# Another order of work around the first expert group of a gated recurrence with four experts

## The chip, the core and the metric

The kernel runs on one core of a Trainium2 chip. The metric is the device time of one launch in microseconds (us): the median over several runs. The engines are TensorE (PE in the profile; PEld is its loading of weights), VectorE (DVE), ScalarE (ACT), GpSimd (POOL) and SyncE (SP), which here only issues DMAs. Each works through its own instructions in order and waits for others by semaphores.

## The reference

Two parts follow each other. The first is a recurrence over time with a matrix as its state (2 batches, 8 heads, 768 steps, 40 features a head); the second feeds its output to four experts, and every expert sees every token.

```python
# recurrence, one step t for every batch and head
m_new  = maximum(f_gate + m, i_gate)
f_stab = exp(f_gate + m - m_new);  i_stab = exp(i_gate - m_new)
C = f_stab * C + i_stab * outer(vt, kt)
n = f_stab * n + i_stab * kt
y[t] = sigmoid(o_gate) * (C @ qt) / maximum(abs(n @ qt), 1.0)
# experts, x is y as 1536 tokens x 320 features
p = domain_probs / (domain_probs.sum(-1) + 1e-9)
out = sum over 4 experts e of  p[:, e] * (relu(x @ w1[e]) @ w2[e])    # hidden width 1024
```

## The kernel before

**Tiling.** The recurrence is computed in 12 chunks of 128 steps (6 a batch; chunk `n` belongs to batch `n % 2`). Within a chunk it is like attention: `scores(n)` (line 435) makes k times q for all heads on TensorE, `weigh(n)` (443) multiplies them on VectorE with decays, `intra(n)` (499) multiplies the weights with the values. What earlier chunks carry comes in by the state: `inter(n)` (480) multiplies q with it, eight ScalarE copies scale the result into `yb` (495), `norm(n)` (508) adds the two on VectorE, applies the output gate and divides. `state(n)` (449) makes the chunk's own part of the state; `carry(n)` (471) scales the old state on GpSimd. `turn(n)` (525) transposes the output on TensorE and ScalarE copies its rounded high part into `xst`; `turn_lo(n)` (535) writes the remainder with VectorE.

**Decays.** `decay(n)` (411) is a VectorE scan over `fb`, the forget factors spread over all partitions. For the first four chunks TensorE spreads them (`spread`, 392); from chunk 4 on a DMA does (`load_f`, 403). The gates themselves are a small chain: `gate_max`, `gate_f`, `gate_i`, `gate_b` (303, a VectorE scan and a ScalarE copy), `gate_t` (320, TensorE transposes of it, copied by ScalarE into `ibT`), `gate_last` (335, GpSimd), `gate_l` (344, TensorE spreads the last values, copied into `bl`). `values(n)` (421) scales the values on GpSimd with `ibT`, and ScalarE writes one more column; `keys(n)` (428) scales the keys on GpSimd. `gate_o(j)` (385) is the sigmoid on ScalarE of two chunks' output gates; it needs another activation table than the exponentials.

**Experts.** For accuracy each of x, w1, w2 is split into a rounded high part and a remainder (`quarter_hi`, `quarter_lo`, `split_w2_hi`, `split_w2_lo`: high on ScalarE, low on GpSimd). `hidden` (152) multiplies 256 tokens with two blocks of w1 in 16 products, then ScalarE writes the relu's high part and VectorE its low part. `output` (191) multiplies with w2. The first expert's work on the first 1024 tokens is cut into four groups of 256 tokens, each a list of steps: four hidden steps and then output steps. The first group has four output steps (high parts of w2 for two tiles of 128 tokens, then low parts), the others two. `steps(n)` (542) emits the next n steps. So expert steps are put by hand between the pieces of the recurrence, where TensorE would otherwise wait.

**Order.** There is no scheduler: the order in which the Python lines run is the order on every engine, and SyncE issues the DMAs in that order too. Lines 548 to 665 are a prologue written out by hand for chunks 0 to 3 and the first four hidden steps; the loop from 667 on does chunks 2 to 11 and takes its number of expert steps at three places of an iteration from `SLOTS` (38): before `inter`, after `weigh(n+1)` and `carry(n+1)`, and a third beside the transposes. Behind the loop come the other tokens and experts, nothing but dense products on TensorE. PSUM buffers come from pools of two: `ps_h` (hidden), `ps_o` (output and spreading), `ps_w` (scores), `ps_y` (chunk outputs, state products, transposes); the next use of a buffer waits for its last reader.

**Zero products.** `keep_warm(n)` (72) multiplies zeros, 128x128 with 128xn, into a buffer nobody reads.

Of the kernel before, what the change touches and what calls it, by code (L numbers as in the profile page):

```python
# [35 lines left out]
NPE = 4  # L36

SLOTS = (
    (0, 2, 0), (1, 1, 0), (1, 1, 0), (1, 1, 0), (1, 1, 0),
    (1, 1, 0), (1, 1, 0), (1, 1, 0), (1, 1, 1), (1, 1, 1),  # L40
)
PAD = 56
# [6 lines left out]
def tile_mlstm_moe(ctx, tc, gt, qk, vk, ot, dp, w1, w2, out):  # L49
# [22 lines left out]
    def keep_warm(n, pool=ps_h, tag="ph"):  # L72

        pwm = pool.tile([L, n], F32, tag=tag, name="pwm")
        nc.tensor.matmul(pwm, zero[:, 0:L], zero[:, 0:n], start=True, stop=True)  # L75
# [32 lines left out]
    def split_w2_hi(ws, f0, n, raw):  # L108
        f = slice(f0, f0 + n)
        split_hi(ws[:, HI, f], raw[:, f])  # L110

    def split_w2_lo(ws, f0, n, raw, eng):
        f = slice(f0, f0 + n)
        split_lo(ws[:, LO, f], ws[:, HI, f], raw[:, f], eng)
# [107 lines left out]
    with ExitStack() as actx:  # L222
# [7 lines left out]
        def quarter_hi(i):  # L230
            f, (ab, c) = slice(i * G, (i + 1) * G), w1r[i]
            split_hi(w1s[:, 0:2, f], ab)
            split_hi(w1s[:, 2, f], c)
# [151 lines left out]
        def gate_o(j):  # L385
            og = acc[:, 2 * j:2 * j + 2]
            nc.scalar.activation(og, og, AF.Sigmoid)
# [4 lines left out]
        def spread(n, pool, tag):  # L392

            b, c, k = n % B, n // B, 48 if n < B else L
            fbs[n] = [pool.tile([L, 4, L], F32, tag=tag, name="fb") for _ in range(2)]
            for h in range(H):
                nc.tensor.matmul(  # L397
                    fbs[n][h // 4][:, h % 4, :],
                    sel[0:k, b * H + h:b * H + h + 1].to_broadcast([k, L]),
                    fr[0:k, c * L:(c + 1) * L], start=True, stop=True,  # L400
                )
# [9 lines left out]
        def decay(n):  # L411
            dds[n] = a1.tile([L, H, L], F32, tag=f"dd{n % 2}", name="dd")
            for i in range(2):
                nc.vector.tensor_tensor_scan(  # L414
                    out=dds[n][:, 4 * i:4 * i + 4].rearrange("p h t -> p (h t)"),
                    data0=fbs[n][i].rearrange("p h t -> p (h t)"),
                    data1=id4.rearrange("p h t -> p (h t)"),
                    initial=0.0, op0=ALU.mult, op1=ALU.add,
                )

        def values(n):
            b, c = n % B, n // B
            vv = vvs[n] = vp[n % 2]
            iec = ibT[:, c, b * H:(b + 1) * H].unsqueeze(2)
            nc.gpsimd.tensor_mul(vv[:, :, 0:D], vks[n // 2][:, n % 2, 0], iec.to_broadcast([L, H, D]))
            nc.scalar.activation(vv[:, :, D:D + 1], iec, AF.Copy)

        def keys(n):
            if n // B < NC - 1:
                nc.gpsimd.tensor_mul(  # L430
                    kp[n % 2][:, :, 0:D], vks[n // 2][:, n % 2, 1],
                    dds[n][:, :, L - 1:L].to_broadcast([L, H, D]),
                )

        def scores(n, pool=ps_w, tag="w"):
            ss[n] = [pool.tile([L, NP, L], F32, tag=tag, name="s") for _ in range(2)]
            qg, kg = qT(n), kT(n)
            for p in range(NP):
                for r in range(2):
                    q = slice(64 * r, 64 + D * r)  # L440
                    nc.tensor.matmul(ss[n][r][:, p, :], kg[q, p], qg[q, p], start=True, stop=True)  # L441
# [100 lines left out]
        def steps(n):  # L542
            for _ in range(n):
                if not work[0].step():
                    work.pop(0)
# [36 lines left out]
        nc.scalar.activation(even, par.unsqueeze(2).to_broadcast([L, 2, 64]), AF.Copy)  # L582
        gate_max(1, NC)
        spread(0, ps_h, "ph")
        scores(0)
        gate_t(0, 1)
        pits.pop(0)
        gate_o(0)
        spread(1, ps_o, "po")
        g1, m1, mp1 = slice(L, S), mb[:, L + 1:S + 1], mb[:, L:S]  # L590
        nc.gpsimd.tensor_add(fs[:, g1], gat[:, 0, g1], mp1)
        decay(0)
        values(0)
        nc.gpsimd.tensor_sub(fs[:, g1], fs[:, g1], m1)
        nc.scalar.activation(fs[:, g1], fs[:, g1], AF.Exp)
        scores(1, ps_h, "ph")
# [9 lines left out]
        nc.sync.dma_start(w2r, w2[0])  # L606
        load_vk(1)
        load_o(1)
        keep_warm(512, ps_w, "w")
        keep_warm(512, ps_w, "w")  # L610
        weigh(1)
        quarter_hi(0)
        quarter_lo(0)
# [8 lines left out]
        turn_lo(1)  # L622
        quarter_lo(1)
        quarter_hi(2)
        keys(0)
        keys(1)
        quarter_lo(2)
        quarter_hi(3)
        quarter_lo(3)
        decay(2)  # L630
        steps(1)
        scores(2)
        weigh(2)
        state(0)
        state(1)
        gate_b(1, NC)
        gate_last(1, NC)
        steps(1)
        spread(3, ps_o, "po")
        decay(3)  # L640
        gate_t(1, NC)
        gate_l(1, NC)
        psum_e = const.tile([L, NCH, 1], F32, name="psum_e")
        nc.gpsimd.tensor_add(psum_e, pw[:, :, 0:1], pw[:, :, 1:2])
        for e in range(2, NE):
            nc.gpsimd.tensor_add(psum_e, psum_e, pw[:, :, e:e + 1])
        nc.gpsimd.tensor_scalar_add(psum_e, psum_e, 1e-9)
        for f in (0, 2):
            split_w2_hi(w2s, f, 2, w2r)
        values(2)  # L650
        carry(2)
        split_w2_lo(w2s, 0, 2, w2r, nc.gpsimd)
        keys(2)
        steps(1)
        for f in (4, 6):
            split_w2_hi(w2s, f, 2, w2r)
        split_w2_lo(w2s, 2, 2, w2r, nc.gpsimd)
        nc.vector.reciprocal(psum_e, psum_e)
        gctx.close()
        a0 = actx.enter_context(  # L660
            tc.tile_pool(name="a0", bufs=1, side="right", reuse_waits="tile")
        )
        load_f(NPE)
        steps(1)
        gate_o(1)

        for n in range(2, NCH):
            j, cc = n // 2, n % 2
            k = SLOTS[n - 2]
            nxt = n + 1 < NCH  # L670
            if cc == 0 and j + 1 < NG:
                load_qk(j + 1)
                load_vk(j + 1)
            if NPE < n + 2 < NCH:
                load_f(n + 2)
            if cc == 0:
                if j > 1:
                    gate_o(j)
                if j + 1 < NG:
                    load_o(j + 1)  # L680
            if n == NCH - 2:
                raw1 = load_w1e(1)
            if n > 2 and nxt:
                decay(n + 1)
            steps(k[0])
            inter(n)
            intra(n)
            norm(n)
            if nxt:
                scores(n + 1)  # L690
            state(n)
            if nxt:
                values(n + 1)
                keys(n + 1)
                weigh(n + 1)
                carry(n + 1)
            if n == 2:
                nc.gpsimd.tensor_mul(pw, pw, psum_e.to_broadcast([L, NCH, NE]))
                for f in (4, 6):
                    split_w2_lo(w2s, f, 2, w2r, nc.gpsimd)  # L700
            steps(k[1])
            if cc == 0:
                steps(k[2])
            turn(n)
            turn_lo(n)
            if cc == 1:
                steps(k[2])
# [109 lines left out]
```

## Time and profile before

| what | value |
|---|---|
| median of 3 runs | 412.97 us (411.39 to 413.19) |
| profiled execution | 414.57 us, its span 412.8 us |
| mean granted TensorE clock | 0.982 |
| PE busy | 403.8 us, 98% of the span |
| DVE busy | 173.6 us, 42% |
| ACT busy | 125.6 us, 30% |
| POOL busy | 82.0 us, 20% |
| DMA | 29.34 MB |

The span runs from the first to the last instruction; the execution's time is a little longer. Busy shares are means over the whole span: the first 60 us, which the change touches, look different from the rest. The profile gives a granted clock for TensorE as a share of 2.4 GHz; at 0.50 the engine runs at 1.2 GHz.

### The profile page before, as it was taken

How to read it: one execution, taken by the hardware profiler on the slowest of the kernel's cores; microseconds unless marked ns; L12 is line 12 of the kernel's file. 1: busy time of each engine (PE TensorE's matmuls, PEld its weight loads, DVE VectorE, ACT ScalarE, POOL GpSimd, SP SyncE). 2: the span in 40 equal slices, each digit the busy share in tenths (PEclk: the TensorE clock that was granted, in tenths of full speed). 3: DMA queues.
4: the chain of work that ended last, by engine and by line, in shares of the span. 5: the costliest groups of instructions: out<-in, count | busy, mean ns of one | idle time of the engine just before them, and what ended most of it. 6: DMA issues, size and time to landing. Idle time of an engine off the chain costs nothing.

```text
span 412.8 us, 7149 instructions
## 1 busy us (share of the span) xinstructions
PE 403.8 (98%) x3036; PEld 364.8 (88%) x3036; DVE 173.6 (42%) x312; ACT 125.6 (30%) x298; POOL 82.0 (20%) x97
## 2 busy tenths in 40 slices
PE   8998999999999999999999999999999999999996
PEld 5788979999998898998988988989989889889896
DVE  8573789798862403313214134133142251231321
ACT  4557334353333533205213033034031140120210
POOL 4849242222011720002510010006100010000000
PEclk9598999999999999999999999999999999999999
DMA  6949095577000112100300004002100000001001
GB/s 175 320 187 253 22 261 117 169 183 253 2 2 2 45 82 91 63 2 0 129 0 2 0 2 152 2 0 74 56 0 2 0 2 32 33 0 49 17 17 48
DMA packets 14884, 29.34 MB, mean 71 GB/s; under 512 B 988, under 2 KB 10748, under 8 KB 13436
## 3 DMA queue, kind: packets, MB, share of 16 engines
q1 hardware_dynamic: 14851, 28.88, 22.5%
q8 instruction: 24, 0.39, 0.4%
q14 instruction: 9, 0.07, 0.1%
HBM read 26.86 MB, written 2.02 MB: 70 GB/s over the span
## 4 chain that ended last, share of the span: by engine, by line
PE 91%; DVE 3%; POOL 2%; DMA 1%; issue 1%; ACT 0%; SPq 0%; DVEq 0%; POOLq 0%
PE po L203 41%; PE ph L164 37%; PE y L503 3%; PE ph L186 3%; PE s L441 3%; PE y L488 2%; DMA qk<-in_qk 1%; POOL w2s L99 1%; PE pwm L75 1%; PE px L530 1%; PE st L459 1%; DVE dd L414 1%; POOL cd L475 0%; DVE pm L447 0%; PE fb L397 0%
## 5 line engine op out<-in xcount | busy, mean ns | idle before, releaser
L203 PE MATMUL po<-w2s,h 128*128 128x320 f32 x1152 | 172.8, 310 | 0.0
L203 PEld LDWEIGHTS po<-w2s,h 128*128 128x128 f32 x1152 | 169.7, 188 | 1.0
L164 PE MATMUL ph<-xst,w1s 128*128 128x512 f32 (+1 forms) x816 | 166.3, 362 | 1.3 <-ACT xst L532 0.9
L164 PEld LDWEIGHTS ph<-xst,w1s 128*128 128x128 f32 x816 | 137.5, 191 | 26.5 <-issue 2.4
L173 ACT ACTIVATE h<-ph 128x512 fp32r<-128x512 f32 x96 | 57.4, 598 | 199.5 <-PE ph L164 199.5
L174 DVE SCALAR_TENSOR_TENSOR h<-ph,h 128x512 fp32r<-128x512 f32 x96 | 66.2, 690 | 104.9 <-ACT h L173 104.4
L213 DVE SCALAR_TENSOR_TENSOR acc<-po,pw,acc 128x320 f32<-128x320 f32 x36 | 19.8, 550 | 99.9 <-PE po L203 99.9
L99 POOL TENSOR_TENSOR w1s<-raw,w1s 128x512 fp32r<-128x512 f32 (+1 forms) x24 | 23.6, 1035 | 74.4 <-ACT w1s L96 67.4
L99 POOL TENSOR_TENSOR w2s<-raw,w2s 128x640 fp32r<-128x640 f32 x6 | 9.5, 1578 | 98.1 <-ACT w2s L96 98.1
L414 DVE TENSOR_TENSOR_SCAN dd<-fb,id 128x512 f32<-128x512 f32 x24 | 28.0, 1209 | 0.3
L495 ACT ACTIVATE yb<-y,ibT 128x41 f32<-128x41 f32 x80 | 16.0, 312 | 2.4 <-PE y L488 2.4
L211 ACT ACTIVATE acc<-po,pw 128x320 f32<-128x320 f32 x12 | 6.3, 528 | 31.7 <-PE po L203 31.7
L441 PE MATMUL s<-qk 64*128 64x128 f32 (+1 forms) x192 | 15.0, 297 | 1.0 <-DMA qk<-in_qk 1.0
L447 DVE TENSOR_TENSOR pm<-s,dd 128x512 f32<-128x512 f32 x24 | 15.4, 686 | 0.6 <-PE s L441 0.3
L503 PEld LDWEIGHTS y<-vp,pm 128*64 128x64 f32 x384 | 13.6, 148 | 1.7 <-issue 1.5
L430 POOL TENSOR_TENSOR kp<-vk,dd 128x320 f32<-128x320 f32 x10 | 7.3, 736 | 37.1 <-DVE dd L414 37.1
L503 PE MATMUL y<-vp,pm 128*64 128x41 f32 x384 | 14.2, 237 | 0.0
L441 PEld LDWEIGHTS s<-qk 64*128 64x128 f32 (+1 forms) x192 | 12.6, 199 | 1.7 <-DMA qk<-in_qk 1.1
L96 ACT ACTIVATE w2s<-raw 128x640 fp32r<-128x640 f32 x12 | 8.8, 733 | 16.4 <-DMA raw<-in_w 16.4
L186 PE MATMUL ph<-xd,w1s 64*128 64x512 f32 x40 | 12.0, 419 | 0.0
L186 PE MATMUL ph<-xst,w1s 64*128 64x512 f32 x40 | 11.9, 417 | 0.0
L96 ACT ACTIVATE w1s<-raw 128x512 fp32r<-128x512 f32 (+1 forms) x24 | 11.2, 516 | 0.0
(90 smaller groups left out, 199.4 us busy)
## 6 DMA issues: line engine op xcount, KB each, us to landing
raw<-in_w SPq DMA_DIRECT2D x3, 1536.0 KB, 6.5
qk<-in_qk SPq DMA_DIRECT2D x5, 832.0 KB
fb<-f_d SPq DMA_DIRECT2D x8, 512.0 KB, 7.1
raw<-in_w SPq DMA_DIRECT2D x3, 1280.0 KB
vk<-in_vk SPq DMA_DIRECT2D x5, 640.0 KB, 9.3
acc<-in_ot SPq DMA_DIRECT2D x6, 320.0 KB, 8.8
out<-acc SPq DMA_DIRECT2D x12, 160.0 KB, 1.8
w2r<-in_w SPq DMA_DIRECT2D x1, 1280.0 KB
```

The costliest lines, as they stand in the source:

```text
L96: nc.scalar.activation(hi, raw, AF.Copy)
L99: eng.tensor_sub(lo, raw, hi.bitcast(F32))
L164: nc.tensor.matmul(ph[:, i, :], self.w1s[:, wi, f * L:(f + 1) * L], xst[:, xi, self.t0:self.t0 + n], start=(k == 0 and not self.wide), sto ...
L173: nc.scalar.activation(hh, ph, AF.Relu)
L174: nc.vector.scalar_tensor_tensor(out=hl, in0=ph, scalar=0.0, in1=hh.bitcast(F32), op0=ALU.max, op1=ALU.subtract)
L186: nc.tensor.matmul(self.banks[f][:, 0, :], self.w1s[r, 5, f * L:(f + 1) * L], x, start=True, stop=False,)
L203: nc.tensor.matmul(po, self.hs[f][a][:, sl], ws[:, b, f, :], start=(first and i == 0), stop=(last and i == len(ks) - 1),)
L213: nc.vector.scalar_tensor_tensor(out=acc[:, i, :], in0=po, scalar=pw[:, i, e:e + 1], in1=acc[:, i, :], op0=ALU.mult, op1=ALU.add,)
L414: nc.vector.tensor_tensor_scan(out=dds[n][:, 4 * i:4 * i + 4].rearrange("p h t -> p (h t)"), data0=fbs[n][i].rearrange("p h t -> p (h t)") ...
L441: nc.tensor.matmul(ss[n][r][:, p, :], kg[q, p], qg[q, p], start=True, stop=True)
L495: nc.scalar.activation(yb[:, h], y1[:, h, 0:D + 1], AF.Copy, scale=ibT[:, c, i:i + 1])
L503: nc.tensor.matmul(y[t, h, 0:D + 1], pms[n][:, h, t], vvs[n][:, h, 0:D + 1], start=True, stop=True,)
```

## The change

Nothing that is computed changes, apart from zero products; instructions are emitted in another order. Two zero products of 256 columns are added between `spread(0)` and `scores(0)`. The two of 512 columns ahead of `intra(1)` become three of 256. `values(0)` stands ahead of `gate_o(0)` (and so its ScalarE column ahead of the sigmoid). `quarter_hi(3)` is called ahead of `keys(0)` and `keys(1)`. `gate_b` and `gate_last` come ahead of the first hidden step, `decay(2)` behind it; `weigh(2)` behind the two states. `gate_t` comes ahead of `spread(3)`, and `gate_l` behind the third hidden step. `gate_o(1)`, `values(2)` and `keys(2)` come ahead of that step. `psum_e`, the sum of the probabilities on GpSimd, comes behind the first low parts of w2 and `carry(2)`, and its reciprocal on VectorE behind the fourth hidden step. The second pair of w2 high parts moves into the loop, behind `norm(2)`. In `SLOTS` chunk 4 takes both its expert steps after its attention.

```diff
--- before.py
+++ after.py
@@ -36,7 +36,7 @@
 NPE = 4
 
 SLOTS = (
-    (0, 2, 0), (1, 1, 0), (1, 1, 0), (1, 1, 0), (1, 1, 0),
+    (0, 2, 0), (1, 1, 0), (0, 2, 0), (1, 1, 0), (1, 1, 0),
     (1, 1, 0), (1, 1, 0), (1, 1, 0), (1, 1, 1), (1, 1, 1),
 )
 PAD = 56
@@ -582,15 +582,17 @@
         nc.scalar.activation(even, par.unsqueeze(2).to_broadcast([L, 2, 64]), AF.Copy)
         gate_max(1, NC)
         spread(0, ps_h, "ph")
+        for _ in range(2):
+            keep_warm(256, ps_w, "w")
         scores(0)
         gate_t(0, 1)
         pits.pop(0)
+        g1, m1, mp1 = slice(L, S), mb[:, L + 1:S + 1], mb[:, L:S]
+        nc.gpsimd.tensor_add(fs[:, g1], gat[:, 0, g1], mp1)
+        values(0)
         gate_o(0)
         spread(1, ps_o, "po")
-        g1, m1, mp1 = slice(L, S), mb[:, L + 1:S + 1], mb[:, L:S]
-        nc.gpsimd.tensor_add(fs[:, g1], gat[:, 0, g1], mp1)
         decay(0)
-        values(0)
         nc.gpsimd.tensor_sub(fs[:, g1], fs[:, g1], m1)
         nc.scalar.activation(fs[:, g1], fs[:, g1], AF.Exp)
         scores(1, ps_h, "ph")
@@ -606,8 +608,8 @@
         nc.sync.dma_start(w2r, w2[0])
         load_vk(1)
         load_o(1)
-        keep_warm(512, ps_w, "w")
-        keep_warm(512, ps_w, "w")
+        for _ in range(3):
+            keep_warm(256, ps_w, "w")
         weigh(1)
         quarter_hi(0)
         quarter_lo(0)
@@ -622,47 +624,45 @@
         turn_lo(1)
         quarter_lo(1)
         quarter_hi(2)
+        quarter_hi(3)
         keys(0)
         keys(1)
         quarter_lo(2)
-        quarter_hi(3)
         quarter_lo(3)
-        decay(2)
-        steps(1)
-        scores(2)
-        weigh(2)
-        state(0)
-        state(1)
         gate_b(1, NC)
         gate_last(1, NC)
         steps(1)
+        decay(2)
+        scores(2)
+        state(0)
+        state(1)
+        weigh(2)
+        steps(1)
+        gate_t(1, NC)
         spread(3, ps_o, "po")
         decay(3)
-        gate_t(1, NC)
+        gate_o(1)
+        values(2)
+        keys(2)
+        steps(1)
         gate_l(1, NC)
+        for f in (0, 2):
+            split_w2_hi(w2s, f, 2, w2r)
+        split_w2_lo(w2s, 0, 2, w2r, nc.gpsimd)
+        carry(2)
+        split_w2_lo(w2s, 2, 2, w2r, nc.gpsimd)
         psum_e = const.tile([L, NCH, 1], F32, name="psum_e")
         nc.gpsimd.tensor_add(psum_e, pw[:, :, 0:1], pw[:, :, 1:2])
         for e in range(2, NE):
             nc.gpsimd.tensor_add(psum_e, psum_e, pw[:, :, e:e + 1])
         nc.gpsimd.tensor_scalar_add(psum_e, psum_e, 1e-9)
-        for f in (0, 2):
-            split_w2_hi(w2s, f, 2, w2r)
-        values(2)
-        carry(2)
-        split_w2_lo(w2s, 0, 2, w2r, nc.gpsimd)
-        keys(2)
-        steps(1)
-        for f in (4, 6):
-            split_w2_hi(w2s, f, 2, w2r)
-        split_w2_lo(w2s, 2, 2, w2r, nc.gpsimd)
-        nc.vector.reciprocal(psum_e, psum_e)
         gctx.close()
         a0 = actx.enter_context(
             tc.tile_pool(name="a0", bufs=1, side="right", reuse_waits="tile")
         )
         load_f(NPE)
         steps(1)
-        gate_o(1)
+        nc.vector.reciprocal(psum_e, psum_e)
 
         for n in range(2, NCH):
             j, cc = n // 2, n % 2
@@ -686,6 +686,9 @@
             inter(n)
             intra(n)
             norm(n)
+            if n == 2:
+                for f in (4, 6):
+                    split_w2_hi(w2s, f, 2, w2r)
             if nxt:
                 scores(n + 1)
             state(n)
```

## Rows read from the trace of the kernel before

**Rows 1.** Stages: busy us (instructions) of each engine, granted clock, DMA share, GB/s.

```profile
60.00:100.00 40.00, 40.00 (x538) 38.42 (x535) 36.00 (x76) 15.43 (x57) 10.44 (x13) 1.00 0.66 183
...
8.50:9.00 0.50, 0.50 (x5) 0.41 (x3) 0.39 (x2) 0.00 (x0) 0.00 (x0) 0.65 1.04 262
...
18.50:19.00 0.50, 0.50 (x17) 0.50 (x16) 0.00 (x0) 0.00 (x0) 0.50 (x1) 0.61 0.89 195
...
24.00:26.00 2.00, 2.00 (x30) 1.75 (x30) 2.00 (x3) 0.73 (x2) 2.00 (x3) 1.00 0.35 141
...
32.50:33.00 0.50, 0.50 (x5) 0.50 (x4) 0.50 (x1) 0.50 (x2) 0.50 (x1) 0.55 0.88 248
```

**Rows 2.** The page's clock line: 40 equal slices of the span, tenths of full clock.

```profile
PEclk9598999999999999999999999999999999999999
```

**Rows 3.** TensorE's timeline to 60 us: start, duration, instructions, idle before and its releaser.

```profile
7.38 1.16 PE L441 MATMUL s<-qk 64*128 64x128 f32 x16 [0.97 <-DMA qk<-in_qk]
...
10.50 2.21 PE L441 MATMUL s<-qk 40*128 40x128 f32 x16
...
14.51 3.78 PE L75 MATMUL pwm<-const-float32-0.0 128*128 128x512 f32 x4
18.22 1.42 PE L503 MATMUL y<-vp,pm 128*64 128x41 f32 x32
...
22.38 2.46 PE L164 MATMUL ph<-xst,w1s 128*128 128x256 f32 x16 [0.47 <-ACT xst L532]
...
26.60 2.16 PE L164 MATMUL ph<-xst,w1s 128*128 128x256 f32 x16
28.60 1.00 PE L397 MATMUL fb<-fr,sel 128*128 128x128 f32 x8
...
31.53 0.39 PE L349 MATMUL pit<-last,even 128*128 128x40 f32 x2 [0.55 <-ACT ibT L331]
31.74 5.56 PE L164 MATMUL ph<-xst,w1s 128*128 128x256 f32 x32
37.23 0.94 PE L488 MATMUL y<-cs,qk 104*64 104x105 f32 x16
38.00 1.08 PE L503 MATMUL y<-vp,pm 128*64 128x41 f32 x32
...
41.63 0.51 PE L459 MATMUL st<-vp,kp 128*40 128x41 f32 x16 [1.45 <-POOL w2s L99]
...
54.30 0.74 PE L164 MATMUL ph<-xst,w1s 128*128 128x256 f32 x4 [0.47 <-ACT xst L532]
```

**Rows 4.** ScalarE's timeline, 14 to 42 us.

```profile
14.39 0.20 ACT L426 ACTIVATE vp<-ibT 128x8 f32<-128x8 f32 x1
...
32.05 1.36 ACT L96 ACTIVATE w2s<-w2r 128x640 fp32r<-128x640 f32 x2
...
38.01 1.28 ACT L387 ACT_TABLE_LOAD   x1
39.30 0.74 ACT L387 ACTIVATE acc<-acc 128x640 f32<-128x640 f32 x1
39.95 1.58 ACT L495 ACTIVATE yb<-y,ibT 128x41 f32<-128x41 f32 x8
```

**Rows 5.** VectorE's timeline, 12 to 55 us.

```profile
12.75 1.29 DVE L447 TENSOR_TENSOR pm<-s,dd 128x512 f32<-128x512 f32 x2 [0.33 <-PE s L441]
...
47.96 0.43 DVE L537 TENSOR_TENSOR xst<-px,xst 128x256 fp32r<-128x256 f32 x1 [2.42 <-ACT xst L533]
...
54.95 0.41 DVE L537 TENSOR_TENSOR xst<-px,xst 128x256 fp32r<-128x256 f32 x1
```

**Rows 6.** GpSimd's timeline, 29 to 35 us.

```profile
29.43 0.51 POOL L646 TENSOR_TENSOR psum_e<-psum_e,pw 128x12 f32<-128x12 f32 x2
...
32.23 1.04 POOL L475 TENSOR_TENSOR cd<-cs,bl 104x512 f32<-104x512 f32 x1
33.23 1.55 POOL L99 TENSOR_TENSOR w2s<-w2r,w2s 128x640 fp32r<-128x640 f32 x1
```

## The prediction

> **What bounds the kernel now.** I read the table of stages and the page's clock line first, then each engine's timeline up to 62 us. From 60 to 100 us TensorE has work for 40.00 of 40 us, VectorE for 36.00 [rows 1]: there TensorE sets the pace, it follows its own order, and what is won ahead of it is kept to the end. The change lies ahead of 60 us, where this is not so. The reader is to see three kinds of loss there.
>
> First the clock. The clock line stands at 5 in its second slice, 8 in its fourth, 9 from the fifth on [rows 2]. In half microseconds: 0.65 in 8.50 to 9.00 means full for 0.15 us and half after it, so the fall is at 8.65; likewise the rise is at 18.89 and the second fall at 32.55 [rows 1]. Half clock doubles products: the second chunk's scores took 2.21 us, the first's 1.16 at full clock [rows 3]. Before the first fall TensorE made eight spreading products, sat idle for 0.97 us and made scores; before the second it made spreading products and the small transposes of the gates, and sat idle for 0.55 [rows 3].
>
> Second, TensorE's own waits: 0.97 for q and k, 0.55 for the gates' last values, 1.45 before the state of chunk 2, 0.47 before expert group 1 [rows 3]. The 1.45 is put down to POOL, but ScalarE's eight `yb` copies ran from 39.95 to 41.53 and the state began at 41.63 [rows 3, 4]; the state product takes the PSUM buffer that these copies read. They stood behind a table load and a sigmoid, 38.01 to 40.04 [rows 4], though the products that they wait for had begun at 37.23 [rows 3].
>
> Third, filler: two zero products of 512 columns at half clock, 14.51 to 18.22, held up `intra(1)`, which could have begun when ScalarE wrote the last column of its values at 14.59 and VectorE its weights at 14.04 [rows 3 to 5].
>
> **Part 1, up to the first hidden step (saves 3.9).** The two products of 256 columns added behind `spread(0)` fall into the 0.97 us of idle. A quarter of the 3.71 us that 1024 columns took at half clock is 0.93, so 256 columns cost 0.93 at half and 0.46 at full clock [rows 3]. Two cost 0.93 (all hidden) to 1.86 (0.89 late). I take 0, since the products just ahead of the gap run at full clock (it falls at 8.65 only). With the gap filled I take the clock to stay full. Then I leave the second scores where they began, 10.50 (their data need not be there before), and add 1.16 for them, 1.08 for `intra(0)` at its full-clock duration, 3 x 0.46 for the three short products: 14.12 [rows 3]. `values(0)` ahead of the sigmoid sets its last column free early, so it does not hold `intra(0)`. Now ScalarE's 14.59 [rows 4] ends last. `intra(1)` begins 18.22 - 14.6 = 3.6 earlier and runs 1.08 instead of 1.42, 0.3 more [rows 3]. Behind it stands the same chain as now: norm(1), turn(1), its copies, the hidden step at 22.38, now 18.5. If the clock stays low the shorter filler alone is left: a quarter of 3.71, 0.93.
>
> **Part 2, four hidden steps (saves 2.35).** Today from 22.38 to 37.23. In it: the first step runs 2.46, the next one, at full clock, 2.16, so 0.3 is lost to VectorE's late low parts; 0.55 of wait for `ibT`; the last two take 5.49 (31.74 to 37.23) instead of 4.0 (twice 26.60 to 28.60), 1.5 lost to the clock [rows 3]. The new order puts `gate_b` ahead of `decay(2)` on VectorE and the transposes ahead of the spreading, with a hidden step between transposes and `gate_l`, so 2.0 us of products cover the `ibT` copy; the second fall has lost its idle time. 0.3 + 0.55 + 1.5 = 2.35. With the fall kept, 0.85.
>
> On data: `scores(2)` comes at about 18.5 + 2.0 = 20.5. No row tells when its q and k land; the transfers as a whole thin out only in 24 to 26 us, 141 GB/s [rows 1]. A wait of 0 to 4 us is the bound; I take 0, because q and k were issued ahead of w2, keys, values and gates of the second group. On SP, `load_f(4)` is released by gate buffers and now comes earlier, with the next q, k, v and gates queued behind it; they stand behind the old transfers and nobody waits for them before the loop.
>
> **Part 3, ScalarE's sigmoid (saves 1.45).** `gate_o(1)` goes ahead of the third hidden step. Its 2.0 us (38.01 to 40.04, [rows 4]) then stand beside spreading and a hidden step, 3 us of products. `yb` can follow its product at once and end 1.9 earlier; the wait of 1.45 goes. Behind the sigmoid on ScalarE are the last value column, the step's relu and the w2 high parts.
>
> The load took 1.28 us and the sigmoid started 0.01 behind it [rows 4]. The Trainium skill, "ScalarE: Activation LUTs", section "What ACT_TABLE_LOAD costs", puts a drain of about 1.38 us on top. By it the relu would be about 0.8 late, use up the margin of part 4, and the total below would shrink by some 0.3; the trace does not bear the drain out here.
>
> **Part 4, w2 parts and the sum of probabilities (0, bounds 0 to -2).** The second pair of w2 high parts goes behind `yb`: 1.36 us [rows 4], while the output step needs them only after four of eight blocks. On POOL `psum_e` goes behind two low parts and a carry, and VectorE's `reciprocal` now stands ahead of `norm(2)` and waits for it. I count: inter(2) comes at 18.5 + (37.23 - 22.38) - 2.35 = 31.0; two us ahead of it, 29.0, the third hidden step is done; `bl` and the first high part take to 29.9; then POOL has 1.55 twice, a carry of 1.04 and four small sums of about 0.25 (two took 0.51): 35.0 [rows 6]. So `norm(2)` starts at 35.2 or so, after the short reciprocal, rather than when `yb` is done (31.0 + 0.9 + 1.6 = 33.5). Behind `norm(2)` and its followers VectorE idled 2.42 before turn_lo(2) [rows 5], so 1.7 of lateness fits, with 0.7 to spare. Without that cover it would cost 1.7. w2's last low part comes at about the time the low output step asks for it; I take 0.5 for this and other joints.
>
> **Part 5, expert group 1 (saves 0.3, bounds 0 to 0.47).** Both steps go behind chunk 4's attention. The step's wait of 0.47 [rows 3] goes, but `intra(4)` needs the PSUM buffer that turn_lo(3) still reads from 54.95 on [rows 5], so VectorE is late there next. I take 0.3. The reordered `quarter_hi(3)` changes no engine's order: 0.
>
> **Sum.** 3.9 + 2.35 + 1.45 + 0.3 - 0.5 = 7.5. The profiled execution took 414.57, 1.77 more than its span, and becomes 407.1. The median shown is 1.60 below it, so I forecast 412.97 - 7.5 = 405.5.
>
> **Rivals.**
> 1. *The clock falls once more* between `intra(1)` and the hidden steps, where TensorE has transposes, spreading and still some idle time. For: just this mix stood before both falls. Against: 1.45 idle at 40 to 41.6 was followed by no fall, since the line stays at 9 [rows 2, 3]. Price 1.5, as two hidden steps paid above: 407.0.
> 2. *The filling doesn't hold the clock*, it falls at 8.65 as before. For: the products around the gap are the same, small ones. Part 1 shrinks from 3.9 to 0.93: 408.5. The Trainium skill, "TensorE: Matmul & The Clock Gate", section "Why this matters for your kernels", warns of idle gaps, but of longer ones than any here; by it the gap wasn't the cause and this rival holds. Against it in this trace: the fall came behind the gap.
> 3. *VectorE becomes late at norm(2)*, through reciprocal and POOL: the margin of 0.7 is missed by 1 to 2 us, 406.5 to 407.5.
> 4. *Slower*: 768 columns at half clock are too few to bring the clock back where 1024 did (rise at 18.89, soon after the last of them, [rows 1, 3]). TensorE goes on at half clock through the hidden steps. From 18.9 to 32 that costs 6.5 us of products, against 0.93 + 0.3 + 0.55 + 1.5 + 1.45 + 0.3 = 5.0 saved: 414.5. It decides from about 10 us of further half clock on. Against: the first fall must come first (rival 2), and hidden steps brought the clock back after the second fall, or the last two would have taken 8, not 5.49.
> 5. *It does nothing*, because waits return elsewhere at equal size: 412 to 413. Against: 60 us onwards nothing but TensorE's own order limits.
>
> **How the numbers follow.** Forecast 0.50, rival 1 0.20, rival 2 0.13, rival 3 0.11, rival 4 0.03, rival 5 0.03. Where the forecast's small terms are off by 2, it reaches 403.5; upwards the range takes in rivals 1 to 3 and 1 us, 409.5. Below 0.5%, 2.1 us, a measurement of this kernel doesn't tell a change from none. Faster: all cases but rivals 4 and 5, 0.94; within: 0.03; slower: 0.03.
>
> **What would show it.** Clock: full from 8.65 to 18.9 (part 1) and around 30 to 33 (part 2); the half-microsecond stages tell. `intra(1)` at about 14.6, first hidden step at 18.5, inter(2) at 31.0, and no wait of the state product on `yb` (part 3). VectorE's reciprocal at about 35, waiting for POOL, and turn_lo(2) still waiting for ScalarE (part 4). Wrong it is if scores(2) waits for its transfer, if half clock shows at 9 to 12 us, or if turn_lo(2) follows weigh(3) without idle time.

## The result, and the profile after

The changed kernel took 410.4 us (median of 20 executions, 407.69 to 413.4); the kernel before, on the same chips, 414.12 (20 executions, 411.39 to 416.62). The ratio is 0.9918, interval 0.989 to 0.9947: 3.4 us less by the ratio (1 - 0.9918 = 0.82% of 414.12; the medians differ by 3.7), where 7.5 were forecast and the range ended at 409.5. So the forecast was wrong in size, although the profiled execution came close to what it said: 407.69 us, where 407.1 was forecast; its span is 405.9 against 412.8, 6.9 less. That execution is the fastest of the 20. An execution more than 1.5% above the fastest of its kernel is left out of the medians and ratios below: one of `before_more_fill` (span 419.5) and two of `best_scan` (415.2; no trace shows why).

TensorE's timeline of it, against [rows 3] (same columns):

```profile
6.54 1.14 PE L75 MATMUL pwm<-const-float32-0.0 128*128 128x256 f32 x4
7.61 1.28 PE L441 MATMUL s<-qk 64*128 64x128 f32 x16
...
10.29 1.16 PE L441 MATMUL s<-qk 64*128 64x128 f32 x16
...
12.44 1.57 PE L75 MATMUL pwm<-const-float32-0.0 128*128 128x256 f32 x6
14.67 1.13 PE L503 MATMUL y<-vp,pm 128*64 128x41 f32 x32 [0.66 <-POOL fr L315]
...
18.46 2.45 PE L164 MATMUL ph<-xst,w1s 128*128 128x256 f32 x16 [0.47 <-ACT xst L532]
...
26.76 2.12 PE L164 MATMUL ph<-xst,w1s 128*128 128x256 f32 x16
28.71 0.31 PE L349 MATMUL pit<-last,even 128*128 128x40 f32 x2
...
30.93 0.94 PE L488 MATMUL y<-cs,qk 104*64 104x105 f32 x16
...
33.81 0.51 PE L459 MATMUL st<-vp,kp 128*40 128x41 f32 x16
...
41.32 0.55 PE L203 MATMUL po<-w2s,h 128*128 128x320 f32 x2 [0.91 <-POOL w2s L99]
...
44.68 0.51 PE L459 MATMUL st<-vp,kp 128*40 128x41 f32 x16
...
49.17 1.13 PE L503 MATMUL y<-vp,pm 128*64 128x41 f32 x32 [1.01 <-DVE xst L538]
...
58.02 0.94 PE L488 MATMUL y<-cs,qk 104*64 104x105 f32 x16
```

The gap for q and k is filled, and 256 zero columns cost 0.52 instead of 0.93 (1.57 / 3 here). `intra(1)` begins at 14.67 (14.6 was forecast; the wait is put down to GpSimd's `fr`, which it does not read, and ScalarE's column below ended at 14.57), the first hidden step at 18.46 (18.5), `inter(2)` at 30.93 (31.0), and the state of chunk 2 no longer waits. New are two waits: 0.91 for w2's last low part at 41.32, 1.01 in `intra(4)` at 49.17. The page's clock line, against [rows 2]:

```profile
PEclk9999999999999999999999999999999999999999
```

ScalarE and VectorE, against [rows 4, 5]: the value column of chunk 1, the `yb` copies with no sigmoid ahead of them, which start at 31.92, right behind their product (30.93 to 31.87), and the reciprocal that waits 3.12 for GpSimd, with turn_lo(2) still idle for 0.50 before it, as part 4 had it.

```profile
14.37 0.20 ACT L426 ACTIVATE vp<-ibT 128x8 f32<-128x8 f32 x1
...
31.10 0.60 ACT L173 ACTIVATE h<-ph 128x512 fp32r<-128x512 f32 x1 [0.18 <-PE ph L164]
31.92 1.59 ACT L495 ACTIVATE yb<-y,ibT 128x41 f32<-128x41 f32 x8 [0.22 <-PE y L488]
```

```profile
19.37 2.47 DVE L306 TENSOR_TENSOR_SCAN gat<-fs,bs 16x640 f32<-16x640 f32 x1
...
35.54 0.23 DVE L665 RECIPROCAL psum_e<-psum_e 128x12 f32<-128x12 f32 x1 [3.12 <-POOL psum_e L658]
...
40.14 0.43 DVE L537 TENSOR_TENSOR xst<-px,xst 128x256 fp32r<-128x256 f32 x1 [0.50 <-ACT xst L533]
```

```profile
19.07 1.43 POOL L430 TENSOR_TENSOR kp<-vk,dd 128x320 f32<-128x320 f32 x2
20.46 2.44 POOL L99 TENSOR_TENSOR w1s<-wa,w1s 128x512 fp32r<-128x512 f32 x1
```

The gate scan at 19.37 took 2.47 us, and GpSimd's low part beside it 2.44. Before, the same two took 1.47 and 1.28, apart from each other:

```profile
27.37 1.47 DVE L306 TENSOR_TENSOR_SCAN gat<-fs,bs 16x640 f32<-16x640 f32 x1
```

```profile
25.01 1.28 POOL L99 TENSOR_TENSOR w1s<-wa,w1s 128x512 fp32r<-128x512 f32 x1
```

The scan ended at 21.84, 1.38 behind the keys' end at about 20.46, and the low part at 22.90, 1.06 behind the scan. So the scan lost 1.0 behind the keys and the low part 1.2 behind the scan. The prediction had no term for that.

### The profile page after: what moved, and what is told of

Read it like the earlier page. It is cut to its first block, busy times and chain, and to the rows that moved or that the text cites. A ratio compares the mean times of both kernels' runs of the same rounds, so it can differ in the third digit from the quotient of the medians.

```text
span 405.9 us, 7159 instructions
## 1 busy us (share of the span) xinstructions
PE 398.3 (98%) x3042; PEld 361.4 (89%) x3042; DVE 175.1 (43%) x312; ACT 125.4 (31%) x298; POOL 83.9 (21%) x97
## 4 chain that ended last, share of the span: by engine, by line
PE 92%; POOL 3%; ACT 2%; DVE 2%; issue 1%; ACTq 0%; DVEq 0%
PE po L203 40%; PE ph L164 39%; PE ph L186 3%; PE s L441 2%; PE y L503 2%; POOL w2s L99 2%; PE y L488 2%; PE pwm L75 1%; PE st L459 1%; PE px L530 1%; PE fb L397 1%; POOL cd L475 0%; ACT yb L495 0%; PE pit L327 0%; ACT L597 0%
## 5 line engine op out<-in xcount | busy, mean ns | idle before, releaser
L164 PE MATMUL ph<-xst,w1s 128*128 128x512 f32 (+1 forms) x816 | 164.3, 359 | 0.5 <-ACT xst L532 0.5
L164 PEld LDWEIGHTS ph<-xst,w1s 128*128 128x128 f32 x816 | 136.0, 189 | 25.0 <-issue 2.4
L503 PE MATMUL y<-vp,pm 128*64 128x41 f32 x384 | 13.2, 229 | 1.7 <-DVE xst L538 1.0
L503 PEld LDWEIGHTS y<-vp,pm 128*64 128x64 f32 x384 | 12.6, 138 | 2.3 <-issue 1.2
L441 PE MATMUL s<-qk 64*128 64x128 f32 (+1 forms) x192 | 14.1, 285 | 0.0
L425 POOL TENSOR_TENSOR vp<-vk,ibT 128x320 f32<-128x320 f32 x12 | 9.6, 798 | 10.6 <-PE st L459 7.7
```

Of the source, the lines that this page charges most:

```text
L164: nc.tensor.matmul(ph[:, i, :], self.w1s[:, wi, f * L:(f + 1) * L], xst[:, xi, self.t0:self.t0 + n], start=(k == 0 and not self.wide), sto ...
L503: nc.tensor.matmul(y[t, h, 0:D + 1], pms[n][:, h, t], vvs[n][:, h, 0:D + 1], start=True, stop=True,)
```

## The experiments

For each execution the span and the mean granted clock are on record, and the study turns on these. Ratios are to executions of the kernel before that were measured beside them.

**Twice the same kernels.** `before_again` and `after_again` are the two kernels unchanged.

> The kernel before, unchanged, for a second trace and for the clock of each of its executions. Theory A (the clock falls at other places from one execution to the next, so the profiled execution of before held more or fewer of these losses than another): spans differ by some 4 us, and follow the mean granted clock, about 0.5 us of span for each us at half clock; the trace has stretches at half clock at other places than 8.65 to 18.89 and 32.55 to 35.96 us. Theory B (the spread comes from when the transfers land): spans differ at equal clock, and the new trace has the stretches at the same places but other waits for q, k or values. Median about 414 by either.

> The changed kernel, unchanged, likewise. Theory A: the profiled execution (span 405.9, clock 0.999) was one of the few in which the clock never fell; most show a clock of 0.988 to 0.996 with a span 1 to 5 us longer, and a new trace shows one or more stretches at half clock between about 9 and 35 us, with the same waits as before. The executions shown with clock 1.0 and a span of 411.5 are then ones that began at half clock and stayed there unrecorded. Theory B: a longer span at a high clock, with longer waits for transfers. Median about 410.4.

Measured: 413.1 (ratio 0.9994, 0.9961 to 1.0027) and 410.76 (0.9939, 0.9903 to 0.9974). The executions fall into groups by clock. The executions of the kernel before are those beside the first twelve experiments and `before_again`'s own (93), the changed kernel's its first 20 and `after_again`'s 12:

| kernel | mean clock shown | executions | span, us |
|---|---|---|---|
| before | 0.990 | 15 | 409.5 to 410.2 |
| before | 0.986 to 0.988 | 24 | 410.8 to 412.0 |
| before | 0.979 to 0.983 | 32 | 412.4 to 414.9 |
| before | 0.994 to 0.996 | 3 | 413.8 to 414.3 |
| before | 0.998 to 1.0 | 19 | 410.7 to 412.7 |
| changed | 0.999 | 3 | 405.9 to 406.2 |
| changed | 0.996 | 6 | 407.0 to 407.6 |
| changed | 0.988 to 0.992 | 15 | 408.2 to 411.0 |
| changed | 1.0 | 8 | 411.4 to 411.6 |

So theory A holds: spans go with the clock, apart from the groups at 0.994 and above in the kernel before and at 1.0 in the changed one (below), and no two executions need agree in it. Theory B, late transfers alone, falls as the cause of the groups, though transfers do land at different times (below), so that theory A's "same waits as before" did not hold. In `after_again` the clock fell although the first gap was filled. Its half-microsecond stages and TensorE's timeline:

```profile
11.50:12.00 0.50, 0.50 (x12) 0.50 (x11) 0.50 (x1) 0.37 (x1) 0.50 (x1) 0.79 1.06 414
...
18.50:19.00 0.50, 0.50 (x18) 0.47 (x14) 0.00 (x0) 0.00 (x0) 0.50 (x2) 0.89 1.01 196
```

```profile
8.83 1.10 PE L397 MATMUL fb<-fr,sel 48*128 48x128 f32 x8
11.20 1.58 PE L441 MATMUL s<-qk 64*128 64x128 f32 x16 [1.27 <-DMA qk<-in_qk]
...
21.76 2.45 PE L164 MATMUL ph<-xst,w1s 128*128 128x256 f32 x16 [0.47 <-ACT xst L532]
```

0.79 in 11.50 to 12.00 puts the fall at 11.79; the rise is at 18.61. Just ahead of the fall TensorE had waited 1.27 for q and k of the second chunk. These came at least 0.9 us later than in the profile after, where the second scores began at 10.29 without a wait. The first hidden step stands at 21.76, 3.3 later than in the profile after.

The last group of the table, clock 1.0 with the longest span, looks like a contradiction. The trace of `before_again` (shown clock 0.999) resolves it:

```profile
5.50:6.00 0.50, 0.50 (x3) 0.50 (x4) 0.50 (x1) 0.00 (x0) 0.00 (x0) 1.00 0.81 197
```

```profile
5.31 1.97 PE L397 MATMUL fb<-fr,sel 48*128 48x128 f32 x8
...
15.24 2.92 PE L75 MATMUL pwm<-const-float32-0.0 128*128 128x512 f32 x4
...
31.31 4.07 PE L164 MATMUL ph<-xst,w1s 128*128 128x256 f32 x32
```

The stage shows 1.00, but the eight spreading products took 1.97 us, their duration at half clock (1.10 at full clock above). The engine was still at half clock there and came up only some time in the zero products at 15.24 (2.92 instead of 3.78 us); the profile shows neither. So a shown 1.00 says nothing of this first stretch. That holds for the trace the prediction was made from too: its opening zero products, 1280 columns from 0.78 on, took 4.60 us, the price of half clock (five times 0.93 is 4.65), under a shown 1.00:

```profile
0.78 4.60 PE L75 MATMUL pwm<-const-float32-0.0 128*128 128x512 f32 x6 [0.78 <-PEq L798]
```

In all 16 kept traces they took 3.80 to 4.61. What differs between executions is when the clock comes up. I infer a late rise for the changed kernel's eight executions of 411.4 to 411.6; none of them was traced.

**Parts of the change.** `fill_only` is the kernel before with part 1 alone, `order_only` the changed kernel with the old zero products, `no_first_fill` the changed kernel without the first two.

```diff
 # fill_only, on before
         spread(0, ps_h, "ph")
+        for _ in range(2):
+            keep_warm(256, ps_w, "w")
         scores(0)
...
+        values(0)
         gate_o(0)
...
-        keep_warm(512, ps_w, "w")
-        keep_warm(512, ps_w, "w")
+        for _ in range(3):
+            keep_warm(256, ps_w, "w")
 # order_only, on the changed kernel: the same two places back
 # no_first_fill, on the changed kernel: the first place back
```

> The kernel before with part 1 of the change alone: two zero products of 256 columns behind the first spreading, three of 256 in the place of two of 512 ahead of intra(1), and values(0) ahead of gate_o(0). By the prediction's sum 3.9 us less than before where the clock holds, 0.9 where it does not. Theory A: some executions with the clock high to about 30 us, a median 1.5 to 2.5 us below before. Theory B: the same 3.9 in each.

> The changed kernel with the zero products of before (none behind the first spreading, two of 512 ahead of intra(1)); all the other moves stay. By the prediction's sum 2.35 + 1.45 + 0.3 - 0.5 = 3.6 less than before where the second fall of the clock goes, 2.1 where it stays. Theory A: median 1.5 to 2.5 us below before, since the moves take waits away (1.45 and 0.55) and add some (0.91 for w2's low part), and what the clock does varies. If the moves are worth the whole measured gain, 3.4 us below before.

> The changed kernel without the two zero products behind the first spreading; the three of 256 columns ahead of intra(1) stay. Theory A (what the fillers are worth hangs on whether the clock is up when they run): where the first products run at full clock, the fill keeps the clock up for 1 to 3 us less loss; where the clock has not come up, each costs 0.93 instead of 0.46 and holds up the scores. The two nearly cancel: median within 1 us of the changed kernel's 410.6, its best executions slower than 405.9 by 2 or more, its slowest faster than 411.6. By the prediction's own working (the fill holds the clock in every execution): 3.0 us slower than the changed kernel.

Measured: `fill_only` 413.24 (0.9989, 0.9959 to 1.0018), no gain that can be told, where theory A had 1.5 to 2.5; `order_only` 411.92 (0.9957, 0.993 to 0.9984), some 1.8; `no_first_fill` 411.03 (0.9939, 0.9919 to 0.9959), the ratio of `after_again`. So part 1, forecast at 3.9 and 3.92 in the profiled execution, is worth about nothing in the median when done alone, and the first fill is worth nothing that can be told. The extremes fit what was expected of theory A: spans of `no_first_fill` lay between 407.9 and 410.5, of the changed kernel between 405.9 and 411.6, as if the fill helped some executions and cost others. The trace of `fill_only` is of one still at half clock there:

```profile
5.31 1.97 PE L397 MATMUL fb<-fr,sel 48*128 48x128 f32 x8
7.21 2.07 PE L75 MATMUL pwm<-const-float32-0.0 128*128 128x256 f32 x4
9.21 2.20 PE L441 MATMUL s<-qk 64*128 64x128 f32 x16
```

Here two fills cost 2.07 and the scores began at 9.21, against 7.61 in the profile after. What a zero product costs and gives hangs on the clock it finds.

**Part 3 alone.** `gate_o_alone` moves one line on the kernel before.

```diff
         gate_l(1, NC)
+        gate_o(1)
...
         load_f(NPE)
         steps(1)
-        gate_o(1)
```

> The kernel before with gate_o(1) moved from the loop's head to behind gate_l, and nothing else: part 3 alone. By the prediction 1.45 us less than before in every execution, whatever the clock does, with the state of chunk 2 no longer behind ScalarE's yb copies. If the wait comes back elsewhere (ScalarE's relu or the w2 parts late): 0 to 0.5 less.

Measured: 412.68 (0.9969, 0.9946 to 0.9992), 1.3 less, with an interval of 0.3 to 2.2; 1.45 was forecast. In the trace it is 0.79: from `inter(2)` to the state 3.61 us (36.62 to 40.23) instead of 4.40 (37.23 to 41.63). The state still waits a little, since ScalarE's second copy of w2's high part (36.81, 1.35 us) and its relu stand ahead of the `yb` copy, which ran from 38.54 to 40.13:

```profile
40.23 0.51 PE L459 MATMUL st<-vp,kp 128*40 128x41 f32 x16 [0.66 <-POOL vp L425]
```

**Part 4's and part 5's waits.** `sums_early` puts the five lines of `psum_e` ahead of `gate_l`; `slots_back` takes the old `SLOTS` entry.

> The changed kernel with the sum of the probabilities on GpSimd put ahead of gate_l, where GpSimd sat idle for 2.58 us. If the wait of 0.91 that TensorE has for w2's last low part is on the path: 0.5 to 0.9 less in every execution with equal clock, the wait gone from the trace. If VectorE's chain sets that stage anyway (decay(4), norm(3)): no change beyond 0.2 at equal clock.

> The changed kernel with the old SLOTS entry: one expert step of chunk 4 ahead of inter(4) again. Part 5 undone. By the prediction 0.3 slower than the changed kernel at equal clock (its executions at 0.990 to 0.992 have spans of 408.2 to 409.3). In the changed kernel intra(4) waits 1.01 for VectorE's turn_lo(3); with the old entry the hidden step should wait 0.47 and 0.38 for the same work. If the two waits are equal in what they cost: within 0.2.

Measured: `sums_early` 409.09 (0.9904, 0.9868 to 0.994). At clock 0.990 to 0.991 its five executions span 407.1 to 407.5, the changed kernel's at 0.990 to 0.992 408.2 to 410.7: 1.1 to 1.5 less (the latter by the changed kernel's median there, 408.8), and the wait of 0.91 is gone from the trace (the eight products run in one piece). From these products' start to the next `inter` it is 1.35 us (41.80 to 43.15) instead of 2.52 (39.29 to 41.81), 1.17 less, so the wait was on the path:

```profile
41.80 1.42 PE L203 MATMUL po<-w2s,h 128*128 128x320 f32 x8
```

`slots_back` 410.75 (0.9927, 0.9897 to 0.9957), the changed kernel within what can be told; an interval of over 2 us can't tell 0.3 from 0. The traces can: from the state of chunk 3 to `inter(5)` it is 13.51 us with the old entry (49.61 to 63.12; before, 51.33 to 64.84) and 13.34 with the new (44.68 to 58.02), so part 5 is worth 0.17. The trace of `slots_back` had more to say: two stretches of half clock, and VectorE's gate scan at 4.51 us.

```profile
20.23 4.51 DVE L306 TENSOR_TENSOR_SCAN gat<-fs,bs 16x640 f32<-16x640 f32 x1
```

```profile
23.36 1.91 POOL L99 TENSOR_TENSOR w1s<-wb,w1s 64x256 fp32r<-64x256 f32 x1
```

```profile
26.69 1.31 PE L327 MATMUL pit<-ident,ib 128*128 128x48 f32 x10 [0.99 <-ACT cs L83]
...
29.15 1.11 PE L397 MATMUL fb<-fr,sel 128*128 128x128 f32 x4 [0.45 <-DVE dd L414]
30.06 3.72 PE L164 MATMUL ph<-xst,w1s 128*128 128x256 f32 x16
```

The scan ended at 24.74. Three low parts of GpSimd passed it at their usual durations (1.28, 0.72 and 1.25, to about 23.37), and the fourth, which takes 0.72 alone, took 1.91. Behind the scan the transposes waited 0.99 and the spreading 0.45, and then the hidden steps ran at half clock, 3.72 instead of 2.12.

**Does the scan's collision cost time?** `lo_behind_scan` puts `gate_b` and `gate_last` ahead of `quarter_lo(2)` and `quarter_lo(3)`, so that GpSimd waits for the scan first.

> The changed kernel with gate_last on GpSimd ahead of the third and fourth quarter's low parts, so that GpSimd waits for VectorE's gate scan and none of its big operations runs beside it. In the changed kernel's trace the scan took 2.47 and the low part beside it 2.44, in slots_back 4.51 and 1.91, alone (before) 1.47 and 1.28. Theory C (the moved scan meets GpSimd's operations and one waits for the other, by chance for long): the scan ends at most 1.5 us behind the keys, no wait of the transposes for the state's copies in the trace; executions at equal clock 0 to 1 us faster, the slowest ones at 0.987 to 0.988 (411.0) gone, mean 0.3 to 0.8 below 410.8. Rival (they run beside each other at no loss on the path): mean unchanged within 0.3.

Measured: 410.23 (0.991, 0.9877 to 0.9943). The scan beside an idle GpSimd took 1.48:

```profile
22.60 1.48 DVE L306 TENSOR_TENSOR_SCAN gat<-fs,bs 16x640 f32<-16x640 f32 x1
```

So the stretching is the collision's. (The 1.91 that the expectation sets beside 1.28 is the small low part, which takes 0.72 alone.) On the time it can't be told: spans at 0.991 to 0.992 are 408.1 to 409.6, those of the changed kernel 408.2 to 410.7, and seven executions are too few for the rare long one. Their mean of 410.07 is 0.8 below the changed kernel's 410.83, as theory C had it, but none of the seven came up late, and without its eight late ones the changed kernel's mean is 410.0. `best_scan`, the same on `best` below:

> The same on best. Theory C: 0 to 0.5 below best's 407.4 to 407.8, spread smaller. Rival: equal.

Measured: 407.1 (four executions; 0.9843, 0.9798 to 0.9888), spans 405.1 to 405.7: from `best` no difference can be told.

**More zero products, in both orders.** `more_fill` is the changed kernel with

```diff
-        for _ in range(2):
+        for _ in range(4):
             keep_warm(256, ps_w, "w")
         scores(0)
...
+        for _ in range(2):
+            keep_warm(256, ps_y, "y")
         scores(1, ps_h, "ph")
...
-        for _ in range(3):
-            keep_warm(256, ps_w, "w")
+        keep_warm(256, ps_w, "w")
         weigh(1)
...
+        keep_warm(128, ps_w, "w")
         turn(1, ps_h, "ph")
...
+        keep_warm(256, ps_w, "w")
         steps(1)
```

and `before_more_fill` has the same in the order of before.

> The changed kernel with zero products of 256 columns 4 (not 2) behind the first spreading, 2 ahead of the second scores, 1 (not 3) ahead of intra(1), 1 ahead of the first hidden step, and one of 128 ahead of turn(1). Theory A: the executions that began at half clock and went on so (span 411.5, clock shown as 1.0) get the clock up earlier, falls between 9 and 20 us get rare: span 406 to 408.5 in most, median 1.5 to 3 us below the changed kernel. Theory B (the spread is the transfers'): the added products only cost, 0.5 to 2 us slower.

> The kernel before in its own order with the zero products of more_fill (4, 2 and 1 of 256, one of 128, one of 256 ahead of the first hidden step). Theory A: the clock is up in most executions until about 30 us, so the gap between this kernel and more_fill (median 409.0) is what the moves are worth at full clock. By the prediction's terms without the clock, 0.55 + 1.45 + 0.3 - 0.5 = 1.8, and 1.5 more where the second fall of the clock stays: 410.8 to 412.3. If the moves gained only by the clock: 409 to 409.5. If the zero products give nothing: 413.7 as before.

Measured: `more_fill` 409.01 (0.989, 0.9853 to 0.9926), no recorded fall in any of six executions, spans 406.3 to 409.0; that is some 1.5 below the changed kernel, but the intervals overlap. Its trace is again of an execution at half clock in the first spreading, and now the clock comes up within the fill:

```profile
5.31 1.97 PE L397 MATMUL fb<-fr,sel 48*128 48x128 f32 x8
7.21 3.51 PE L75 MATMUL pwm<-const-float32-0.0 128*128 128x256 f32 x8
...
12.22 1.10 PE L397 MATMUL fb<-fr,sel 48*128 48x128 f32 x8
```

1024 columns took 3.51 (3.78 at half, 2.01 in an execution at full clock) and the next spreading 1.10. `before_more_fill` gained nothing that can be told: 413.5 (0.9986, 0.9954 to 1.0017), 4.5 above `more_fill` (4.0 by the ratios). In its trace the clock was full from the fill until 29.56 and then fell twice, each time behind TensorE's waits that the new order takes away:

```profile
29.50:30.00 0.50, 0.50 (x4) 0.50 (x4) 0.50 (x2) 0.50 (x2) 0.46 (x2) 0.56 1.07 282
...
39.50:40.00 0.50, 0.50 (x12) 0.45 (x6) 0.47 (x3) 0.00 (x0) 0.50 (x1) 0.80 0.00 0
```

```profile
27.21 1.31 PE L327 MATMUL pit<-ident,ib 128*128 128x48 f32 x10 [0.79 <-ACT ib L310]
29.08 0.39 PE L349 MATMUL pit<-last,even 128*128 128x40 f32 x2 [0.55 <-ACT ibT L331]
...
39.18 0.51 PE L459 MATMUL st<-vp,kp 128*40 128x41 f32 x16 [1.45 <-POOL w2s L99]
39.62 6.50 PE L203 MATMUL po<-w2s,h 128*128 128x320 f32 x32
```

So the moves are worth some 4 with these zero products and 1.8 with the old ones (`order_only`), and the zero products some 2.8 in the new order (0.9957 to 0.989) and nothing that can be told in the old. In this trace the moves of parts 2 and 3 have both to gain, the waits and the clock lost behind them. Here the 1.45 us of idle was followed by a fall, at 39.80; in the trace of before, by which rival 1 was weighed, it was not.

**Together.** `best` is `more_fill` with `sums_early`; `best_ph` moves chunk 3's transposes to the hidden steps' PSUM pool as well (`turn(n, *((ps_h, "ph") if n == 3 else ()))`).

> more_fill and sums_early together. At equal clock sums_early was about 1.2 below the changed kernel, and more_fill had its median at 409.0: 407.8 to 408.2 if the two add, 408.8 if VectorE's chain takes the first back.

> As best, and chunk 3's transposes go to the PSUM pool of the hidden steps, so that intra(4) doesn't wait for turn_lo(3) to read its buffer. The wait of 1.01 shrinks to what weigh(4) leaves, some 0.3: 0.5 to 0.7 below best. If VectorE is late anyway behind it: within 0.2 of best.

Measured: `best` 407.38 (0.9843, 0.9803 to 0.9883), 3 below the changed kernel; `best_ph` 408.7 (0.9864, 0.9827 to 0.9901), not the 0.5 to 0.7 below `best` that was expected; the two can't be told apart. In `best_ph` the wait of 1.01 shrank to 0.19, but the next hidden group then waits 0.58 for VectorE:

```profile
47.76 1.02 PE L503 MATMUL y<-vp,pm 128*64 128x41 f32 x28 [0.19 <-DVE pm L447]
...
55.23 2.17 PE L164 MATMUL ph<-xst,w1s 128*128 128x256 f32 x16 [0.58 <-DVE h L174]
```

Its fastest span, 405.2, is also `best`'s: with TensorE's wait moved to another result of VectorE, VectorE sets this stage, as the prediction's part 5 had feared.

## Why the prediction was wrong

The step that failed is in part 1: "With the gap filled I take the clock to stay full." It was given 0.50 as the forecast, with 0.20 for one more fall. Of the changed kernel's 32 executions in the table 3 show no fall (0.999), 6 show a short stretch at half clock (0.996), 15 a longer one, and 8 seem to have come up late. The forecast described the best execution, and that the profiled one was it is luck; the median lies in the third group. `after_again`, with 410.95 near the median, shows the sum term by term (us saved against the trace of before):

| part | from, to | forecast | profile after | `after_again` |
|---|---|---|---|---|
| 1 | start, first hidden step | 3.9 | 3.92 | 0.62 |
| 2 | first hidden step, `inter(2)` | 2.35 | 2.38 | 2.44 |
| 3 | `inter(2)`, state of chunk 2 | 1.45 | 1.52 | 1.52 |
| 4 | state of chunk 2, state of chunk 3 | -0.5 | -1.17 | -1.17 |
| 5 | state of chunk 3, `inter(5)` | 0.3 | 0.17 | 0.17 |
| sum | | 7.5 | 6.82 | 3.58 |
| spans differ by | | | 6.9 | 3.6 |

So part 1 was taken 3.3 too high for the common execution, and part 4's cost 0.7 too low. The base adds to it: 412.97 was the median of three executions, 1.15 below the 414.12 of twenty. Beside [rows 3] the table needs one line of before:

```profile
51.33 0.51 PE L459 MATMUL st<-vp,kp 128*40 128x41 f32 x16
```

Two facts stand behind part 1. First, the sum was taken from one trace of before, with falls at 8.65 and 32.55. The clock differs from execution to execution of the same program: `before_again` has it down from the start and no second fall. The Trainium skill, "TensorE: Matmul & The Clock Gate", section "What's actually happening", says that where the clock comes up varies between runs of one kernel. The runs here agree, with spans of 405.9 to 411.6 for one program; I had not used it. Second, the gap of 0.97 was not the only one. Part 1 said that the second q and k "need not be there before" 10.50; TensorE at full clock stood before them at 9.93 (`after_again`), and waited 0.28 to 1.71 in four traces of the new order with the first gap filled (`after_again`, `slots_back`, `sums_early`, `lo_behind_scan`). In all four the clock fell behind or in that stretch, at 10.45 to 11.91. That the wait causes the fall is not shown by itself: `more_fill` put products there, and added others too. What makes the clock fall stays open.

The steps one by one:

- Part 1: 3.92 (22.38 to 18.46) where the clock holds, 0.62 (22.38 to 21.76) in `after_again`; the prediction's own figure for a clock that stays low was 0.93. In the median of `fill_only` about 0.
- Part 2: 37.23 - 22.38 = 14.85 became 30.93 - 18.46 = 12.47, so 2.38; forecast 2.35. Of this 1.5 is the second fall: in `before_again`, which has none, the stretch took 13.36 (21.95 to 35.31, its last two hidden steps 4.07), and 0.9 is left, the prediction's 0.85. `scores(2)` waited for its transfer in one trace only, 0.73 in `best`. All the moves together, without the new zero products, are worth some 1.8 in the median (`order_only`).
- Part 3: from `inter(2)` to the state 4.40 became 2.88, so 1.52; forecast 1.45. Right together with part 4's move of the second pair of w2 high parts: alone it is 0.79 in the trace of `gate_o_alone`, so that the 1.3 of its median is near 1.45 partly by luck. The state's wait is gone in every kept trace of the new order.
- Part 4: forecast 0 with 0.5 for joints. VectorE's margin held (0.50 left of the 0.7). The low part cost more: the wait of 0.91 on TensorE, 1.17 in the trace, and 1.1 to 1.5 in the spans of `sums_early`.
- Part 5: forecast 0.3, measured 0.17 (13.51 - 13.34). `intra(4)` waits 1.01 for turn_lo(3), the cause as given.

3.92 + 2.38 + 1.52 = 7.82; the spans differ by 6.9, so parts 4 and 5 together took 0.9 back, where 0.2 (0.5 - 0.3) was forecast. Apart from the clock in part 1 and the size of part 4's wait the mechanism was right.

Rival 2 comes nearest: the clock does fall with the gap filled, though behind another wait, and part 1 shrinks to 0.62 where it had 0.93. Its 408.5 was 1.9 too low, of which 1.15 is the base and about 0.7 part 4. Rival 1's size is that of the six executions at 0.996 (spans 407.0 to 407.6, some 409 in time); none was traced, so where their clock fell is not known. Rival 4 shows in no trace: in the four traces named above the clock was up again at 15.33 to 18.61, ahead of the first hidden step; the eight executions of 411.4 to 411.6 are without a trace. Rival 3 did not occur in the profiled execution.

## What to carry to other kernels

Where TensorE's clock falls or comes up in a kernel's first tens of microseconds, one trace is one draw: list span and granted clock of many executions before a term is taken from it, and give the forecast to the common case and not to the clean one. Check the first products' durations against the shown clock, because these traces show a start at half clock as 1.00. Here zero products paid only in the order that had lost its waits; so take waits away first (part 3's one moved line gave 1.3 in the median), then fill what is left.

## What the runs showed of the hardware

VectorE's gate scan, which reads two SBUF operands, and GpSimd's two-operand instructions hold each other up when both are ready: the scan took 1.47 apart, and beside them 2.42 to 2.47 in eight traces of the new order and 4.51 in one; the large low part took 1.28 apart and 2.44 beside the scan, the small one 0.72 and 1.91. In each trace of such a meeting the scan ended 1.3 to 1.4 behind the end of a GpSimd instruction, as if it had begun only there, and the next GpSimd instruction ended 0.5 to 1.1 behind the scan. The Trainium skill, "GPSIMD Engine Reference", section "1. Specifications", names contention with VectorE instructions of two SBUF inputs; the traces agree, and the scan stood behind two GpSimd instructions in one (profile after) and three in another (`slots_back`). The transfers of q and k for chunk 1 were waited for until between 10.27 and 11.64 in four traces of the new order whose kernels do not differ up to there.
